# Attention and two feed-forward layers on one core: probabilities transposed in two halves of 64 queries

## The chip, the cores and the metric

The kernel runs on one core of one Trainium2 chip. The metric is the device time of one execution in microseconds (us); the kernel before takes 1026.38 us, the median of 3 runs (1026.12 to 1026.88).

## What is computed

Four batches of eight heads, 576 positions, head size 64. Attention keeps only the scores within `tau` of a row's largest, and its output feeds two feed-forward layers (512 to 2048 to 512) over the 2304 tokens; all of it in float32.

```python
scores = scale * (q @ k^T)
scores = where(scores >= max(scores) - tau, scores, -1e9)
attn   = softmax(scores) @ v              # x: 2304 tokens x 512
x = gelu_like(x @ w_in1) @ w_out1         # h / (1 + exp(-1.702 h))
x = mish(x @ w_in2) @ w_out2
```

## The kernel before, in words

**Attention.** A program of 72 groups. A "full" group is 128 queries of a pair of heads (two heads, 64 channels each, stacked on the 128 partitions); a "mix" group gathers the last 64 queries of the heads of two pairs. For a group TensorE computes the scores (line 628) into two two-bank PSUM tiles `sc`, one for each head, with 64 rows of the array for each head. VectorE scales them and takes the row's minimum (line 651, it also empties `sc`), GpSimd adds `tau` (line 655), ScalarE takes the exponential (line 658), and VectorE applies the mask and sums (line 661). The probabilities lie with queries on the partitions in `pair` (tiles `g0a` to `g3a` in the trace).

**Turning and the product.** The product with v contracts over keys, so the probabilities are transposed first. `turn` (from line 682) issues this for a group in three units: four transposes of 128 x 128 into bank `tb[0]`, four into `tb[1]` (both line 702), and one for the last keys of both heads into `tb[2]` (line 697). Each unit is followed by a ScalarE copy out of PSUM (line 717): 128x512, 128x512, 128x128, into `pm` (tiles `wout1a`, `wout2a`) and `pmt` (`g0a`, `g1a`). `product` (line 740) runs once for two full groups: 20 matmuls of 256 columns into one half of `tb[3]`, in an array shape of 128 rows by 64 columns, and a ScalarE copy (line 749). `product_mix` (line 765) does the same for a mix group with 64 columns, and its result is copied out by line 772.

**Three array shapes.** Scores use 64 rows x 128 columns of the array for each matmul (64x64 in mix groups), transposes 128x128, products 128x64. Every change between them is a change of the array's shape.

**The feed-forward layers.** 48 steps (24 a layer); a step has seven products of line 867 into `h` and 48 matmuls of lines 942 and 945 (layer 1) or 987 (layer 2). `h` lies in the banks of `sc` and can be opened only when the last scores are read. The weights arrive as 64-bit words and are converted on ScalarE, VectorE and GpSimd (lines 414 to 428), then split in two float32r parts (lines 481, 482, 486, 503, 504); the activations are split in the same way (lines 531, 556, 557, 561). The conversion of layer 1 is done once, in its first eight steps and ahead of them.

**What sets the order.** `Order` is a list scheduler written by hand. Every operation is added with an engine, a planned duration, the keys that it reads and writes, and a rank; the scheduler runs a small event model and issues each engine's instructions in the order that the model gives. `NUDGE` shifts the ranks of single operations by their number. `KEEP` and `TURN` are the model's preference for staying in an array shape (`mode`) and its charge for a change. Softmax work has the rank of its group; the conversion of weights and the loading of the first activations have late ranks, so on VectorE they fill what the softmax leaves open. Keys are per bank: an operation that writes `("tb", 0)` is put behind the copy that reads it.

```python
add("PE", n * 0.109, lambda bank=bank, cs=cs: tr(bank, cs),
    ps, [("tb", bank)], rank, steps=max(n, 2))
add("ACT", t_act(cols), lambda src=src, dst=dst: nc.scalar.copy(dst, src),
    [("tb", bank)], [kpn + (half,)], rank)
```

## Time and profile before

| what | value |
|---|---|
| median of 3 runs | 1026.38 us (1026.12 to 1026.88) |
| the profiled execution | 1026.8 us |
| its span in the trace | 1025.0 us |
| TensorE busy (PE) | 1018.3 us, 99% |
| VectorE busy (DVE) | 831.7 us, 81% |
| ScalarE busy (ACT) | 660.0 us, 64% |
| GpSimd busy (POOL) | 170.2 us, 17% |
| granted TensorE clock | 0.999 of full speed |

PE is matmuls and PEld the loads of their stationary operand, which overlap them. A matmul's recorded duration holds its way through the array, so several overlap and a busy PE row is no proof of an engine at its limit; the distance from one start to the next tells the pace. In the timeline of an engine, `x8` means eight instructions merged in one row, with the time from the first start to the last end. Attention fills the first 260 us or so, the feed-forward layers the rest.

### The profile page before, as it was taken

What the parts mean: (1) busy time and instruction counts of PE and PEld (TensorE: products, weight loads), DVE (VectorE), ACT (ScalarE), POOL (GpSimd) and SP (SyncE); (2) the same over time, 40 slices, a digit from 0 to 9 for tenths busy, and PEclk for the clock granted to TensorE, in tenths of its full rate; (3) what the DMA queues carried; (4) which work ended last, traced back from release to release, by engine and by line L of the source; (5) the groups of instructions that cost most, each with busy time, mean ns of one, the idle gap of its engine ahead of it and who ended that gap; (6) DMA issues with size and microseconds to landing.
All of it is one profiled execution on the core that took longest, in us unless ns stands there. A gap on an engine that the chain in (4) does not pass through costs nothing.

```text
span 1025.0 us, 17308 instructions
## 1 busy us (share of the span) xinstructions
PE 1018.3 (99%) x6362; PEld 866.5 (85%) x6362; DVE 831.7 (81%) x1642; ACT 660.0 (64%) x1262; POOL 170.2 (17%) x182
## 2 busy tenths in 40 slices
PE   9999999999999999999999999999999999999998
PEld 6666666666899999999999999989988998989897
DVE  6999999999889999888887788866597665985643
ACT  5888788888966778666777567644364444544430
POOL 2344444333221211112221012000000000000000
PEclk9999999999999999999999999999999999999999
DMA  5442437532246637755375543611135122131101
GB/s 198 135 137 76 142 117 244 175 96 76 87 154 200 205 122 262 245 209 197 110 273 192 206 171 101 220 64 62 63 104 164 62 73 72 62 124 62 42 1 62
DMA packets 55366, 137.52 MB, mean 134 GB/s; under 512 B 8433, under 2 KB 18673, under 8 KB 55281
## 3 DMA queue, kind: packets, MB, share of 16 engines
q1 hardware_dynamic: 55280, 136.41, 39.7%
q8 instruction: 50, 0.82, 0.3%
q14 instruction: 36, 0.29, 0.1%
HBM read 105.38 MB, written 31.01 MB: 133 GB/s over the span
## 4 chain that ended last, share of the span: by engine, by line
PE 97%; DVE 1%; ACT 1%; issue 0%; POOL 0%; POOLq 0%; DVEq 0%; ACTq 0%
PE h L867 34%; PE tb L987 13%; PE tb L942 13%; PE sc L628 8%; PE tb L740 7%; PE h L945 7%; PE h L987 6%; PE tb L702 6%; PE tb L697 1%; PE tb L765 1%; PE tb L579 1%; DVE win2a L651 0%; ACT wout1a L717 0%; ACT g2a L658 0%; DVE g0a L661 0%
## 5 line engine op out<-in xcount | busy, mean ns | idle before, releaser
L881 DVE TENSOR_TENSOR hs<-h,u 128x384 f32<-128x384 f32 x144 | 79.8, 554 | 88.9 <-PE h L867 55.6
L867 PE MATMUL h<-xq,win 128*128 128x384 f32 x672 | 131.9, 335 | 0.0
L867 PE MATMUL h<-xq,win2b 128*128 128x384 f32 x672 | 131.7, 335 | 0.0
L867 PE MATMUL h<-xq,win1b 128*128 128x384 f32 x672 | 131.1, 335 | 0.0
L867 PEld LDWEIGHTS h<-xq,win1b 128*128 128x128 f32 x672 | 116.2, 188 | 5.5 <-ACT u L889 0.3
L867 PEld LDWEIGHTS h<-xq,win2b 128*128 128x128 f32 x672 | 116.2, 188 | 5.4
L867 PEld LDWEIGHTS h<-xq,win 128*128 128x128 f32 x672 | 115.7, 188 | 5.0 <-ACT u L889 0.5
L651 DVE TENSOR_SCALAR_CACHE_REDUCE win2a<-sc,nqsc 128x576 f32<-128x576 f32 x144 | 112.0, 812 | 5.5 <-PE sc L628 5.1
L889 ACT COPY u<-h 128x384 f32<-128x384 f32 x144 | 68.7, 477 | 72.7 <-PE h L867 71.6
L884 ACT ACTIVATE hs<-hs 128x384 f32<-128x384 f32 x144 | 75.7, 526 | 60.3 <-DVE hs L881 58.9
L655 POOL TENSOR_SCALAR nm<-nm,tau_p 128x1 f32<-128x1 f32 x144 | 84.2, 586 | 159.8 <-DVE win2a L651 156.5
L628 PE MATMUL sc<-win1a 64*128 64x288 f32 (+3 forms) x672 | 90.3, 415 | 0.5 <-DVE win2a L651 0.5
L486 DVE TENSOR_TENSOR sv<-sv 128x256 f32<-128x256 f32 x192 | 80.3, 419 | 1.3
L426 POOL TENSOR_TENSOR sg<-sg,sr 128x1024 uint32<-128x1024 uint32 x16 | 42.5, 2655 | 215.0 <-DVE sg L423 125.1
L628 PEld LDWEIGHTS sc<-win1a 64*128 64x128 f32 (+1 forms) x672 | 50.9, 174 | 28.6 <-issue 10.0
L481 ACT CAST win1b<-sv 128x256 fp32r<-128x256 f32 (+1 forms) x96 | 42.0, 442 | 44.0 <-DVE sv L486 26.2
L481 ACT CAST win<-sv 128x256 fp32r<-128x256 f32 (+1 forms) x96 | 42.3, 443 | 38.4 <-DVE sv L486 26.8
L481 ACT CAST win2b<-sv 128x256 fp32r<-128x256 f32 (+1 forms) x96 | 42.2, 445 | 29.6 <-DVE sv L486 19.7
L482 DVE TENSOR_TENSOR win<-sv,win 128x256 fp32r<-128x256 f32 (+1 forms) x96 | 50.6, 532 | 10.4 <-ACT win L481 10.4
L426 POOL TENSOR_TENSOR sv<-sv,sr 128x1024 uint32<-128x1024 uint32 x16 | 43.0, 2685 | 79.0 <-DVE sv L423 44.7
L482 DVE TENSOR_TENSOR win1b<-sv,win1b 128x256 fp32r<-128x256 f32 (+1 forms) x96 | 48.2, 506 | 7.5 <-ACT win1b L481 7.3
L482 DVE TENSOR_TENSOR win2b<-sv,win2b 128x256 fp32r<-128x256 f32 (+1 forms) x96 | 46.3, 483 | 9.8 <-ACT win2b L481 9.5
(244 smaller groups left out, 2285.9 us busy)
## 6 DMA issues: line engine op xcount, KB each, us to landing
sv<-w_d SPq DMA_DIRECT2D x80, 512.0 KB
sr<-in_w_in SPq DMA_DIRECT2D x16, 1024.0 KB
sr<-in_w_out SPq DMA_DIRECT2D x32, 512.0 KB
win1a<-in_kq SPq DMA_DIRECT2D x16, 576.0 KB
xr<-x_d SPq DMA_DIRECT2D x24, 384.0 KB
w_d<-sv SPq DMA_DIRECT2D x16, 512.0 KB
w_d<-sg SPq DMA_DIRECT2D x16, 512.0 KB
x_d<-xo SPq DMA_DIRECT2D x16, 288.0 KB
```

Source lines behind the costliest of these rows:

```text
L426: lambda: nc.gpsimd.tensor_tensor(bits, bits, word(0), ALU.add), keys, [kval], rank, port=True)
L481: add("ACT", t_act(256 * m, psum=False), lambda: nc.scalar.copy(at(0), src), [ku] + pre_in, keys, rank)
L482: add("DVE", t_dve(256 * m), lambda: nc.vector.tensor_tensor(at(1), src, at(0), ALU.subtract), [ku], keys, rank, port=True)
L486: add("DVE", t_dve(256), lambda: nc.vector.tensor_tensor(out, x, y, op), [], [ku], rank, port=True)
L628: nc.tensor.matmul(sc[i][at:at + m, g, c0:c0 + n], kq2[rows, q0:q0 + m], kq2[rows, k0:k0 + n], start=True, stop=True)
L651: lambda: nc.vector.tensor_scalar(n3, s3, nqsc, None, ALU.mult, ALU.min, accum_out=nm[:, 0:1]),
L655: lambda: nc.gpsimd.tensor_scalar(nm[:, 1:2], nm[:, 0:1], tau_p, 0.0, ALU.add, ALU.add),
L867: nc.tensor.matmul(dst(), w[:, h, c], xq[p][:, x, cs], start=(start and i == 0), stop=(p in (5, 6) and i == 5), skip_group_check=True)
L881: add("DVE", t_dve(HALF), lambda: nc.vector.tensor_tensor(ht[:, cs], x(), y, ALU.add), [kx, ky], [kh + (j,)], rank - 4.0)
L884: lambda: nc.scalar.activation(ht[:, cs], x() if y is None else ht[:, cs], fn),
L942: nc.tensor.matmul(acc2[e](), w[:, x], g(y)[:, 0:512], start=first, stop=last, skip_group_check=True)
L987: nc.tensor.matmul(acc2[t](), g(x)[:, t * 128:(t + 1) * 128], w[:, y], start=(k == i == j == 0), stop=(k == KP - 1 and i == 1 and j == 2), ...
```

## The change

The nine transposes of a group become eighteen, each of 64 queries: half `r` reads 64 partitions of `pair` and multiplies by a 64 x 64 corner of the identity, so it uses the array in the shape of the scores (64 rows x 128 columns). The sixteen main ones are one unit, with the two halves in turn; half 0 goes to bank `tb[0]`, half 1 to `tb[1]`. The tail is a second unit, with its halves in `tb[2]` and `tb[3]`. The copies are two of 128x512 (in blocks of 64 queries) and two of 128x64. The results of the product go alternately to `tb[2]` and `tb[3]`, beside the tails; `pm` becomes two buffers of 2048 columns in place of four of 1024. The transposes get the scores' `mode` in the scheduler, and `NUDGE` is another table.

```diff
--- before.py
+++ after.py
@@ -44,36 +44,43 @@
 NUDGE = {
-    14: 7, 26: -2, 43: 53, 54: -34, 59: -17, 67: -3, 70: -1, 80: -3, 86: -5, 87: -32, 116: 49, 121:
...
+    10: 37, 16: 8, 37: -5, 46: -1, 53: -1, 55: -29, 62: 8, 66: -38, 73: 4, 83: 14, 85: 30, 93: -48,
...
 }
@@ -588,7 +595,7 @@
     nms = Ring(mpool, "nm", 8, [128, 2], F32)
     sms = Ring(mpool, "sm", 4, [128, 32], F32)
     rts = Ring(mpool, "rt", 2, [128, 32], F32)
-    pms = Ring(cut("wout", 1, 2, 1024) + cut("wout", 2, 2, 1024), "pm", 4)
+    pms = Ring([early["wout", 1], early["wout", 2]], "pm", 2)
     pmt = Ring([early["g", i][:, 1168:1424] for i in range(2)], "pmt", 2)
     xos = Ring(mpool, "xo", 3, [128, S], F32)
     xo = {}
@@ -688,34 +695,40 @@
             xo[b, hp] = xos.next()
         half = t % 2 if full else 0
         if not full or t % 2 == 0:
-            turned[b, hp] = [pms.next(), pms.next(), pmt.next()]
-        plan = [(0, (0, 1)), (1, (2, 3)), (2, (4,))]
-
-        def tr(bank, cs):
-            for n, c in enumerate(cs):
-                if c == 4:
-                    nc.tensor.transpose(tb[bank][:, 0:128], pair[:, 516:644], ident)
+            turned[b, hp] = [pms.next(), pmt.next()]
+        (pm, kpm), (rest, krest) = turned[b, hp]
+
+        def tr(out, at, r):
+            rows = slice(64 * r, 64 * r + 64)
+            nc.tensor.transpose(out, pair[rows, at:at + 128], ident[rows, rows])
+
+        def block(k, r):
+            tr(tb[r][:, 64 * k:64 * k + 64], (P1 + 64 if k % 2 else 4) + k // 2 * 128, r)
+
+        def main():
+            for k in range(8):
+                for r in range(2):
+                    block(k, r)
                     yield
-                    continue
-                for i in range(len(ps)):
-                    a, c0 = (P1 + 64 if i else 4) + c * 128, (n * len(ps) + i) * 128
-                    nc.tensor.transpose(tb[bank][:, c0:c0 + 128], pair[:, a:a + 128], ident)
-                    yield
-
-        for (bank, cs), (pn, kpn) in zip(plan, turned[b, hp]):
-            n = 1 if 4 in cs else len(ps) * len(cs)
-            cols = 128 * n
-            n = add("PE", n * 0.109, lambda bank=bank, cs=cs: tr(bank, cs),
-                ps, [("tb", bank)], rank, steps=max(n, 2))
-            if sch.fill is None and WARM:
-                sch.fill = ("PE", n, 0.107, keep_warm)
-            src = tb[bank][:, 0:cols]
-            dst = pn[:, 0:cols]
-            if full:
-                dst = pn.rearrange("p (g q) -> p g q", q=256)[:, :, half * 128:half * 128 + 128]
-                src = src.rearrange("p (g q) -> p g q", q=128)
-            add("ACT", t_act(cols), lambda src=src, dst=dst: nc.scalar.copy(dst, src),
-                [("tb", bank)], [kpn + (half,)], rank)
+
+        def tail():
+            for r in range(2):
+                tr(tb[2 + r][:, 0:64], 516, r)
+                yield
+
+        n = add("PE", 8 * 0.109, main, ps, [("tb", 0), ("tb", 1)], rank, steps=16, mode=1)
+        add("PE", 0.109, tail, ps, [("tb", 2), ("tb", 3)], rank, steps=2, mode=1)
+        if sch.fill is None and WARM:
+            sch.fill = ("PE", n, 0.107, keep_warm)
+        for r in range(2):
+            dst = pm.rearrange("p (g q) -> p g q", q=256)[:, :, half * 128 + 64 * r:half * 128 + 64 * r + 64]
+            src = tb[r].rearrange("p (g q) -> p g q", q=64)
+            add("ACT", t_act(512), lambda src=src, dst=dst: nc.scalar.copy(dst, src),
+                [("tb", r)], [kpm + (2 * half + r,)], rank)
+        for r in range(2):
+            at = half * 128 + 64 * r
+            add("ACT", t_act(64), lambda r=r, at=at: nc.scalar.copy(rest[:, at:at + 64], tb[2 + r][:, 0:64]),
+                [("tb", 2 + r)], [krest + (2 * half + r,)], rank)
         if not full:
             for i in range(2):
                 product_mix(b, hp - 1 + i, i, turned[b, hp], rank)
@@ -727,23 +740,24 @@
         _, b, hp, t = tl
         _, vr, _, kvr = head[b, hp]
         at = t // 2 * 256
-        pn = [p for p, _ in turned[b, hp]]
+        (pm, kpm), (rest, krest) = turned[b, hp]
         i = avn[0] % 2
         avn[0] += 1
-        av, kav = tb[3][:, i * 256:i * 256 + 256], ("tb", 3)
+        av, kav = tb[2 + i][:, 64:320], ("tb", 2 + i)
 
         def mm(cs):
             for c in cs:
                 for i in range(2):
-                    p, a = (pn[c // 2], (c % 2 * 2 + i) * 256) if c < 4 else (pn[2], 0)
+                    p, a = (pm, (c * 2 + i) * 256) if c < 4 else (rest, 0)
                     vc = c * 128 + 64 * i
                     nc.tensor.matmul(
                         av[64 * i:64 * i + 64], vr[:, vc:vc + 64], p[:, a:a + 256],
                         start=(c == 0), stop=(c == 4))
                     yield
 
-        for cs, (_, kp) in zip(((0, 1), (2, 3), (4,)), turned[b, hp]):
-            add("PE", len(cs) * 0.43, lambda cs=cs: mm(cs), [kp + (0,), kp + (1,), kvr], [kav, "product"],
+        for cs, kp in (((0, 1), [kpm + (i,) for i in range(4)]), ((2, 3), [kpm + (i,) for i in range(4)]),
+                       ((4,), [krest + (i,) for i in range(4)])):
+            add("PE", len(cs) * 0.43, lambda cs=cs: mm(cs), kp + [kvr], [kav, "product"],
                 rank + VR, steps=2 * len(cs), mode=2)
         x, kx = xo[b, hp]
         add("ACT", t_act(256), lambda: nc.scalar.copy(x[:, at:at + 256], av), [kav],
@@ -752,22 +766,23 @@
     def product_mix(b, hp, i, pn, rank):
 
         _, vr, _, kvr = head[b, hp]
-        av, kav = tb[2][:, 256 + 64 * i:320 + 64 * i], ("tb", 2)
+        (pm, kpm), (rest, krest) = pn
+        av, kav = tb[2][:, 320 + 64 * i:384 + 64 * i], ("tb", 2)
 
         def mm():
             for c in range(5):
                 for j in range(2):
                     q = 64 * (j ^ i)
                     if c < 4:
-                        p, a, vc = pn[c // 2][0], (c % 2 * 2 + i) * 128 + q, c * 128 + 64 * j
+                        p, a, vc = pm, (c * 2 + i) * 256 + q, c * 128 + 64 * j
                     else:
-                        p, a, vc = pn[2][0], q, 512 + 64 * (i if i == j else 2 + i)
+                        p, a, vc = rest, q, 512 + 64 * (i if i == j else 2 + i)
                     nc.tensor.matmul(
                         av[64 * j:64 * j + 64], vr[:, vc:vc + 64], p[:, a:a + 64],
                         start=(c == 0), stop=(c == 4))
                 yield
 
-        add("PE", 0.575, mm, [k + (0,) for _, k in pn] + [kvr], [kav], rank + VR, steps=5, mode=2)
+        add("PE", 0.575, mm, [kpm + (0,), kpm + (1,), krest + (0,), krest + (1,), kvr], [kav], rank + VR, steps=5, mode=2)
         x, kx = xo[b, hp]
         add("ACT", t_act(64), lambda: nc.scalar.copy(x[:, 512:S], av), [kav], [kx + (4,)], rank + VR)
         finish(b, hp, rank + VR)
@@ -829,7 +844,7 @@
     reopen("win", 1, [("kq", i) for i in range(3)])
     reopen("win", 2, [("ss", i) for i in range(NSS)])
     for i in range(2):
-        reopen("wout", 1 + i, [("pm", 2 * i), ("pm", 2 * i + 1)])
+        reopen("wout", 1 + i, [("pm", i)])
     for i in range(4):
         reopen("g", i, [("p", i)] + ([("pmt", i)] if i < 2 else []))
     for i in range(3):
```

## Rows read from the trace of the kernel before

**Rows 1.** The page: span, busy time by engine, and shares of the chain.

```profile
span 1025.0 us, 17308 instructions
PE 1018.3 (99%) x6362; PEld 866.5 (85%) x6362; DVE 831.7 (81%) x1642; ACT 660.0 (64%) x1262; POOL 170.2 (17%) x182
...
PE 97%; DVE 1%; ACT 1%; issue 0%; POOL 0%; POOLq 0%; DVEq 0%; ACTq 0%
```

**Rows 2.** Busy time by stretch: length, PE, PEld, DVE, ACT, POOL, clock, DMA share, GB/s.

```profile
20.00:40.00 20.00, 19.02 (x152) 11.98 (x151) 19.73 (x50) 17.68 (x32) 7.24 (x12) 1.00 0.17 59
40.00:240.00 200.00, 200.00 (x1753) 131.57 (x1752) 197.60 (x509) 167.35 (x337) 81.31 (x116) 1.00 0.43 141
240.00:280.00 40.00, 40.00 (x364) 29.95 (x363) 37.14 (x88) 36.40 (x75) 11.23 (x15) 1.00 0.31 90
280.00:400.00 120.00, 120.00 (x694) 112.45 (x693) 111.04 (x166) 85.96 (x150) 23.35 (x9) 1.00 0.55 180
400.00:480.00 80.00, 80.00 (x462) 74.72 (x461) 67.84 (x113) 57.07 (x107) 15.69 (x6) 1.00 0.64 217
```

**Rows 3.** Groups of VectorE instructions from 0 to 250 us.

```profile
L651 DVE TENSOR_SCALAR_CACHE_REDUCE win2a<-sc,nqsc 128x576 f32<-128x576 f32 x136 | 105.8, 812 | 5.5 <-PE sc L628 5.1
...
L428 DVE SCALAR_TENSOR_TENSOR sv<-sr,sv 128x1024 uint32<-128x1024 uint32 x6 | 7.3, 1214 | 0.0
L557 DVE TENSOR_TENSOR xq<-xr,xq 128x768 fp32r<-128x768 f32 x5 | 4.8, 952 | 0.0
```

**Rows 4.** TensorE timeline, 12 to 263 us: start, time, engine, line, operation.

```profile
12.05 1.24 PE L628 MATMUL sc<-win1a 64*128 64x288 f32 x8
13.22 1.09 PE L702 MATMUL tb<-ident,g0a 128*128 128x128 f32 x8
...
256.37 1.24 PE L628 MATMUL sc<-win1a 64*128 64x288 f32 x8
257.54 0.33 PE L697 MATMUL tb<-ident,g0a 128*128 128x128 f32 x1
257.70 1.04 PE L702 MATMUL tb<-ident,g0a 128*128 128x128 f32 x8
258.58 0.27 PE L697 MATMUL tb<-ident,g1a 128*128 128x128 f32 x1
258.78 1.08 PE L740 MATMUL tb<-wout1a,x22a 128*64 128x256 f32 x8
```

**Rows 5.** TensorE timeline, 262 to 270 us: products, transposes, feed-forward matmuls.

```profile
262.39 1.95 PE L740 MATMUL tb<-wout2a,x20a 128*64 128x256 f32 x16
264.17 0.60 PE L740 MATMUL tb<-g1a,x20a 128*64 128x256 f32 x4
264.70 0.33 PE L697 MATMUL tb<-ident,g2a 128*128 128x128 f32 x1
...
265.66 1.29 PE L867 MATMUL h<-xq,win 128*128 128x384 f32 x6
266.79 0.60 PE L702 MATMUL tb<-ident,g3a 128*128 128x128 f32 x4
267.22 0.27 PE L697 MATMUL tb<-ident,g3a 128*128 128x128 f32 x1
```

**Rows 6.** TensorE timeline, 272 to 274 us: a mix product, 64 columns a matmul.

```profile
272.43 0.69 PE L765 MATMUL tb<-wout2a,x22a 128*64 128x64 f32 x16
272.95 0.29 PE L765 MATMUL tb<-g1a,x22a 128*64 128x64 f32 x4
```

**Rows 7.** Loads of the stationary operand, from 120.82 us: the scores' first four.

```profile
120.82 0.30 PEld L628 LDWEIGHTS sc<-win1a 64*128 64x128 f32 x4 [0.39 <-DVE sv L420]
```

**Rows 8.** Groups of ScalarE instructions from 0 to 250 us.

```profile
L717 ACT COPY wout2a<-tb 128x512 f32<-128x512 f32 x66 | 37.1, 595 | 10.0 <-PE tb L702 9.7 <-ACT wout2a L717 0.2
...
L717 ACT COPY g0a<-tb 128x128 f32<-128x128 f32 x32 | 8.9, 278 | 2.7 <-PE tb L697 2.7
...
L772 ACT COPY xo<-tb 128x64 f32<-128x64 f32 x14 | 2.9, 210 | 1.5 <-PE tb L765 1.4
```

**Rows 9.** ScalarE timeline, 126 to 130 us: two copies, then two exponentials.

```profile
126.81 1.07 ACT L717 COPY wout2a<-tb 128x512 f32<-128x512 f32 x2
...
127.91 1.48 ACT L658 ACTIVATE g1a<-win2a,nm 128x576 f32<-128x576 f32 x2
```

**Rows 10.** The waits from 0 to 250 us: who, on whom, total us, times, longest.

```profile
PEld tb L702 <- ACT wout1a L717: 2.8, 7, 0.6
```

65 rows, old and new, of the table NUDGE are left out of this document.

## The prediction

> **What bounds the kernel now.** I read the page first. TensorE is busy for 99% of the span and holds 97% of the chain that ended last [rows 1]. That alone proves little, since recorded matmuls overlap, so I looked at starts in TensorE's timeline. Where a run of one kind ends, the next begins at once, and the same distance recurs [rows 4, 5]; the largest wait of a transpose on a copy sums to 2.8 us in the first 250 us [rows 10]. TensorE really has no holes there.
>
> The table by stretch shows a second full engine. From 40 to 240 us VectorE is busy for 197.60 of 200 us (98.8%) while the attention runs, and from 280 to 400 us, where the first eight feed-forward steps and the conversion of layer 1's weights lie, for 111.04 of 120 [rows 2]. The reader is to see that both engines are packed until about 400 us, and that only behind it (67.84 of 80 from 400 to 480) VectorE has room. Part of what VectorE does in the attention is filler: weight conversion and the first activations [rows 3], which are needed for the feed-forward steps and have been pulled forward. So time that TensorE gives back shows in the end only as far as VectorE can follow: its mandatory softmax must move closer together, and the filler must be done later.
>
> **The change part by part, TensorE.** A run of ten transposes starts at 257.54 and is followed by a product at 258.78: 1.24 us. Its middle eight take 0.88 from first start to the next kind's start, 0.110 each, so ten would be 1.10; the other 0.14 lie at the two ends, 0.07 an end [rows 4]. Where transposes follow feed-forward matmuls of the same 128x128 shape, four of them take 0.43, 0.108 each, and the first costs nothing extra [rows 5]. So what the ends cost is the change of shape. A change ends one run and begins another, two ends, 0.14 us, if the scores' ends cost what the transposes' do. I counted 65 changes between the scores' 64x128 and the transposes' 128x128 (24 of them from transposes back to scores), from the one ahead of 13.22 to the one ahead of 257.54 [rows 4]. With the new shape these go: 65 x 0.14 = 9.1 us. The others (transposes or products on one side, products or mix scores on the other) stay in this order; another order may have fewer, which I don't count.
>
> The transposes themselves: nine at 0.110 = 0.99 us a group become nine pairs. What a pair costs no row shows. It streams 64 columns in each half; in a mix product two 64-column matmuls side by side take 0.065 (eight pairs from 272.43 to 272.95) [rows 6]. That is the low end, 0.59 us a group, a gain of 0.40 or 29 us over 72 groups. The high end is that the two halves don't overlap and each keeps a transpose's pace, 0.22 a pair, a loss of 0.99 a group or 71 us. For overlap speak the scores, in the very shape that is used: their first four loads of a 64x128 operand take 0.30 us from first start to last end [rows 7], less than three transposes take, and eight matmuls of 288 columns take 1.17 [rows 4], 0.146 each against 0.110 for 128 columns in a transpose. I take 0.110 a pair, no gain and no loss, which is also what the scheduler charges, and between the ends it is close to the low one; the gain that may lie below it is one that VectorE would not let through (below).
>
> A rule speaks against this change. The Trainium skill, "TensorE: Matmul & The Clock Gate", section "LDWEIGHTS (loading the stationary operand)", says that a load costs its columns at 1.2 GHz whatever the number of rows, so a half-height load costs as much as a full one, 107 ns. Eighteen loads one behind the other would be 1.92 us a group by it, an estimate, and the sum would come out some 60 us slower; with the two row halves loaded side by side it would be 0.96, about what there is now. The overlap in [rows 7] speaks for the second.
>
> **ScalarE.** The two 512-column copies stay at 0.595 each; one of 128 columns (0.278) becomes two of 64 (0.210 by the copy of a mix result, the nearest row), 0.142 more a group, 10.2 us in all [rows 8]. ScalarE is busy for 167.35 of 200 us [rows 2], so 72 groups' addition fits, and I cost it at nothing; the cover is its 33 us of idle time there. Blocks of 64 queries in place of 128 may slow the copies; the bound is nothing to a tenth of two copies, 0.12 us a group, also inside the cover.
>
> **Order and buffers.** Before, the first copy ran while the second bank was filled. Now both banks fill together, so both copies begin at the end of the run, and the next run waits for both. Behind it on TensorE would stand scores, and behind these VectorE's first softmax step. Between two runs TensorE has a group's scores (1.17 us [rows 4]) and half of a product (20 matmuls from 262.39 to 264.70, so 1.16 [rows 5]), 2.33 together; two copies take 1.07 [rows 9]. That hides it, with 1.26 us to spare, and costs nothing in the forecast. The product's first quarter now needs all four copies of two groups rather than two; it is issued a group and a half later, so nothing waits. The tails and the results of products share `tb[2]` and `tb[3]`, but products have two banks in place of one; I set it at nothing. `pm` keeps its size. No DMA is added or moved by hand; VectorE's and GpSimd's instructions are the same in number and size.
>
> **VectorE's limit, and the sum.** VectorE idles 2.67 us from 20 to 240, 2.86 from 240 to 280 and 8.96 from 280 to 400 [rows 2]: 14.5 us is all that could go before its deadline work ends, the upper bound. At the density that it holds now (98.8%), the 365.5 us of work from 20 to 400 need 370.0, a gain of 10.0. But part of its idle time behind 280 is waiting for `h` in the feed-forward chain; if half of that stays, the gain is 2.4 (20 to 280 at that density) + 4.5 = 6.9. I take the middle, 8.5, just under the 9.1 that TensorE gives. The profiled execution took 1026.8 us, 1.8 around its span and 0.4 over the median: 1026.8 - 8.5 = 1018.3, which is 1017.9 against the median.
>
> **Rivals.**
> 1. *More comes through* (0.13). Pairs run at 0.065 and another order drops more changes, so TensorE has up to 38 us to give, and VectorE's filler moves behind 400 us. Then the bound is its idle time up to 480: 14.5 + 12.2 = 26.6 us [rows 2], so 1000 to 1012. For it: the mix product's pace. Against: weight conversions have their deadlines in those first steps.
> 2. *The gain is lost on the way* (0.12). TensorE finishes the attention earlier and then stands in the first feed-forward steps, because the filler that VectorE skipped is late for the weights of steps 1 to 7; or 64-query copies lengthen ScalarE's queue. The time is then 1022 to 1028. For it: VectorE's 92.5% from 280 to 400. Mostly within 0.2%.
> 3. *Both banks at once make TensorE wait* (0.10, slower). If ScalarE has two exponentials ahead of the two copies (1.48 us [rows 9]), bank and copies take 2.55, 0.22 over what TensorE has in between; 72 times is 16 us, less 9.1 is 7 slower: 1033. It decides as soon as the wait is over 9.1 / 72 = 0.13 us a group. Against: TensorE hardly waits for copies now [rows 10], and the scheduler sees this dependence.
> 4. *The halves don't overlap* (0.05, slower). 71 - 9 = 62 us slower, 1088; the change then doesn't do what its shape promises. The Trainium skill's rule on loads, above, is this case when the loads come one behind the other. Against it: [rows 7].
>
> **How the numbers follow.** The forecast has 0.60, with 1012 to 1022 for itself (all of VectorE's idle time down to a third of it). The range leaves out rivals 3 and 4 (0.15) and the far part of rival 1: 1006 to 1027. A measurement of this kernel tells about 0.2%, 2 us, from no change. Faster by more: the forecast, rival 1 and a part of rival 2, 0.78; within: the rest of rival 2, 0.07, and a sliver of rival 3, 0.08; slower: the others, 0.14.
>
> **What would show it.** Right: 18 transposes a group of 64x128 at 0.11 a pair or less, no extra 0.07 between scores and transposes, the first feed-forward matmul (265.66 now [rows 5]) some 6 to 10 us earlier, VectorE at 98 to 99% until about 390. If VectorE instead shows idle time in the attention with transposes as releaser, or transposes waiting for copies, rival 3 holds; if pairs start 0.22 apart, rival 4; if TensorE shows holes from 260 to 400, rival 2. My prediction is wrong if VectorE is no limit, that is, if the gain goes past 15 us, or if the attention gets no shorter although the shape changes are gone.

## The result, and the profile after

The changed kernel takes 1034.21 us (1033.06 to 1039.16 over 3 runs), 1.0086 times the kernel before, interval 1.0073 to 1.01. The forecast was 1017.9 us and faster; it is 8 us slower and lies outside the range. Line numbers have moved: scores 628 to 635, first softmax step 651 to 658, exponential 658 to 665, second step 661 to 668, transposes to 703, their copies to 726 (512 columns) and 730 (64), product 740 to 753 and its copy 749 to 763, mix product 765 to 780, feed-forward products 867 to 882 and 942 to 957.

The page after, against [rows 1]: span, busy time, chain, and the scores' group (busy, mean ns, then idle time before it and what ended it).

```profile
span 1032.4 us, 18739 instructions
PE 1003.7 (97%) x7010; PEld 859.3 (83%) x7010; DVE 829.5 (80%) x1642; ACT 662.9 (64%) x1334; POOL 168.0 (16%) x182
...
PE 82%; DVE 7%; ACT 6%; issue 3%; DMA 2%; DVEq 0%; POOL 0%; SPq 0%; ACTq 0%; POOLq 0%
...
L635 PE MATMUL sc<-win1a 64*128 64x288 f32 (+3 forms) x672 | 107.4, 415 | 14.8 <-DVE win2a L658 14.2
```

TensorE's share of the chain fell from 97% to 82%, and VectorE and ScalarE have come in. The same stretches as in [rows 2]:

```profile
20.00:40.00 20.00, 17.23 (x190) 10.54 (x188) 17.69 (x48) 18.42 (x37) 7.84 (x13) 1.00 0.18 61
40.00:240.00 200.00, 182.96 (x2199) 123.35 (x2198) 195.90 (x499) 165.16 (x379) 77.74 (x115) 1.00 0.45 145
240.00:280.00 40.00, 37.09 (x432) 26.29 (x428) 37.19 (x96) 34.61 (x87) 9.29 (x14) 1.00 0.25 76
280.00:400.00 120.00, 120.00 (x724) 111.34 (x721) 101.29 (x156) 88.03 (x153) 26.74 (x10) 1.00 0.48 160
400.00:480.00 80.00, 80.00 (x463) 74.88 (x462) 69.66 (x110) 56.48 (x106) 15.34 (x6) 1.00 0.62 216
```

The second column is TensorE, the fourth VectorE. From 40 to 240 us TensorE now has 17.0 us of idle time and had none; VectorE has 4.1 us where it had 2.4. Over 20 to 280 us VectorE's idle time grew from 5.5 to 9.2 us. TensorE was relieved and the attention got no shorter. The waits from 0 to 290 us say where TensorE's new idle time lies (the forms of [rows 10]):

```profile
PEld sc L635 <- DVE win2a L658: 29.9, 56, 2.5
...
PE sc L635 <- DVE win2a L658: 14.2, 20, 2.4
...
PEld tb L703 <- ACT wout1a L726: 3.0, 7, 1.3
...
PE tb L753 <- ACT g1a L730: 2.3, 2, 1.2
...
PE tb L703 <- ACT xo L763: 2.2, 4, 0.8
```

Before, from 0 to 250 us, the first of these was

```profile
PEld sc L628 <- DVE win2a L651: 6.7, 20, 0.8
```

Scores wait for VectorE to empty the bank, 29.9 us at the loads and 14.2 at the matmuls. Transposes waiting for the copies of the probabilities stay as small as they were (3.0 us here, 2.8 before, in the largest row of each). Two waits are new and smaller: products for the copies of the tails (line 730, 2.3 us), and transposes for the copies of products (line 763, 2.2 us), with which they now share banks. TensorE's timeline after, near the end of the attention:

```profile
254.89 0.67 PE L703 MATMUL tb<-ident,g1a 64*128 64x64 f32 x16
255.39 0.37 PE L703 MATMUL tb<-ident,g0a 64*128 64x64 f32 x2
256.79 1.97 PE L635 MATMUL sc<-win1a 64*128 64x288 f32 x8 [1.02 <-DVE win2a L658]
...
267.43 2.36 PE L882 MATMUL h<-xq,win 128*128 128x384 f32 x12
...
277.94 0.66 PE L703 MATMUL tb<-ident,g3a 64*128 64x64 f32 x16
278.69 1.95 PE L753 MATMUL tb<-wout1a,x20a 128*64 128x256 f32 x16
280.47 0.60 PE L753 MATMUL tb<-g0a,x20a 128*64 128x256 f32 x4
...
285.70 0.69 PE L780 MATMUL tb<-wout2a,x20a 128*64 128x64 f32 x16
286.22 0.29 PE L780 MATMUL tb<-g1a,x20a 128*64 128x64 f32 x4
286.44 0.50 PE L957 MATMUL tb<-g0b,wout 128*128 128x512 f32 x1
```

And before, the same places:

```profile
269.20 0.60 PE L740 MATMUL tb<-g0a,x20a 128*64 128x256 f32 x4
...
275.45 0.69 PE L765 MATMUL tb<-wout2a,x20a 128*64 128x64 f32 x16
...
280.50 0.39 PE L942 MATMUL tb<-g0b,wout 128*128 128x512 f32 x1
```

Sixteen half transposes from 254.89 are followed by the next kind at 255.39: 0.50 us, eight pairs at 0.062. The first feed-forward product starts at 267.43 (265.66 in [rows 5]), 1.8 later. But the last product of full groups reaches its last four matmuls at 280.47 where it reached them at 269.20, 11.3 later, and the last mix product starts at 285.70 instead of 275.45, 10.3 later. The first output matmul (line 957, 942 before) needs the hidden products of its step, which TensorE does between these remains of the attention; it starts at 286.44 instead of 280.50, 5.9 later.

To say where time goes I read the same events from each kernel's timelines (us): the start of the last first softmax step (A, line 651 or 658), the last second step (B), the first feed-forward product (H), the first output matmul (O), the first output matmul of the ninth step, behind layer 1's conversion (O9), and the last output matmul of all (E).

| kernel | A | B | H | O | O to O9 | O9 to E |
|---|---|---|---|---|---|---|
| before | 262.8 | 265.2 | 265.7 | 280.5 | 127.1 | 613.4 |
| after | 263.7 | 270.8 | 267.4 | 286.4 | 127.2 | 614.7 |
| b_plain | 265.8 | 268.3 | 268.8 | 285.3 | 130.1 | 615.1 |
| b_merge_plain | 269.0 | 275.0 | 271.1 | 291.3 | 127.7 | 615.6 |
| b_sf4_plain | 266.4 | 268.9 | 269.4 | 285.9 | 129.8 | 614.8 |
| a_plain | 268.5 | 277.8 | 269.3 | 293.7 | 123.9 | 617.0 |
| a_cost_plain | 258.7 | 265.9 | 261.3 | 280.5 | 132.8 | 616.9 |
| a_sf4_plain | 260.1 | 263.4 | 261.0 | 278.6 | 133.3 | 617.5 |
| a_half_plain | 257.5 | 266.4 | 259.9 | 279.7 | 135.1 | 616.9 |
| a_cost_ranked | 258.0 | 263.4 | 258.8 | 277.0 | 126.7 | 616.8 |
| a_sf4_ranked | 260.4 | 265.1 | 261.3 | 280.1 | 126.1 | 614.7 |

Of the 7.3 us by which E comes later after the change, 5.9 lie ahead of O, 0.1 between O and O9, and 1.3 behind. Ahead of O the first softmax steps end almost when they did (0.9 later); the rest is a longer tail behind them. The mean distance from a group's first to its second softmax step (each time the later of its two) grew from 3.7 to 7.3 us, and from there to the product (from the second of its two full groups) from 6.9 to 10.4. So the attention is a pipeline of almost the same pace that has become 7.1 us deeper, and a deeper pipeline takes longer to run empty: behind A there are 74 half transposes (four groups) and 60 product matmuls of full groups left, before it was 18 transposes (two groups) and 36. From A to O, before and after:

```profile
262.84:280.50 17.66, 17.66 (x151) 14.98 (x147) 14.98 (x35) 17.01 (x36) 3.86 (x3) 1.00 0.29 93
263.73:286.44 22.71, 21.78 (x229) 16.37 (x223) 19.18 (x46) 22.51 (x55) 1.92 (x3) 1.00 0.11 36
```

TensorE is all but full there, and ScalarE, with the copies and exponentials of those groups, is busy for 22.51 of 22.71 us; so what is left of the attention holds up the feed-forward steps. H, O and O9 say when one kind of work first starts, and the order decides what is done around them; only A and E tell how far the whole has come.

### The profile page after: what moved, and what is told of

It is laid out like the page before. It is cut to its first block, busy times and chain, and to the rows that moved or that the text cites. A ratio compares the mean times of both kernels' runs of the same rounds, so it can differ in the third digit from the quotient of the medians.

```text
span 1032.4 us, 18739 instructions
## 1 busy us (share of the span) xinstructions
PE 1003.7 (97%) x7010; PEld 859.3 (83%) x7010; DVE 829.5 (80%) x1642; ACT 662.9 (64%) x1334; POOL 168.0 (16%) x182
## 4 chain that ended last, share of the span: by engine, by line
PE 82%; DVE 7%; ACT 6%; issue 3%; DMA 2%; DVEq 0%; POOL 0%; SPq 0%; ACTq 0%; POOLq 0%
PE h L882 33%; PE tb L1002 13%; PE tb L957 12%; PE h L1002 6%; PE h L960 6%; PE sc L635 5%; PE tb L753 4%; DVE win2a L658 3%; PE tb L703 2%; DMA sr<-in_w_in 1%; ACT g2a L665 1%; ACT wout1a L726 1%; ACT g1a L665 1%; DVE g3a L668 1%; ACT wout2a L726 1%
## 5 line engine op out<-in xcount | busy, mean ns | idle before, releaser
L635 PE MATMUL sc<-win1a 64*128 64x288 f32 (+3 forms) x672 | 107.4, 415 | 14.8 <-DVE win2a L658 14.2
L635 PEld LDWEIGHTS sc<-win1a 64*128 64x128 f32 (+1 forms) x672 | 60.1, 174 | 41.6 <-DVE win2a L658 29.9
L493 DVE TENSOR_TENSOR sv<-sv 128x256 f32<-128x256 f32 x192 | 84.1, 439 | 1.4
L488 ACT CAST win<-sv 128x256 fp32r<-128x256 f32 (+1 forms) x96 | 42.3, 444 | 44.8 <-DVE sv L493 29.9
L489 DVE TENSOR_TENSOR win2b<-sv,win2b 128x256 fp32r<-128x256 f32 (+1 forms) x96 | 49.8, 522 | 9.9 <-ACT win2b L488 9.5
```

The lines of the kernel that those rows point to most:

```text
L488: add("ACT", t_act(256 * m, psum=False), lambda: nc.scalar.copy(at(0), src), [ku] + pre_in, keys, rank)
L489: add("DVE", t_dve(256 * m), lambda: nc.vector.tensor_tensor(at(1), src, at(0), ALU.subtract), [ku], keys, rank, port=True)
L493: add("DVE", t_dve(256), lambda: nc.vector.tensor_tensor(out, x, y, op), [], [ku], rank, port=True)
L635: nc.tensor.matmul(sc[i][at:at + m, g, c0:c0 + n], kq2[rows, q0:q0 + m], kq2[rows, k0:k0 + n], start=True, stop=True)
```

## The experiments

There were two questions: which engine carries the attention now, and what made the pipeline deeper. Each ratio is against the kernel before, run on the same chip (medians of 1026.4 to 1027.4 us).

### Which engine carries it

**pe_before** and **pe_after**: more tail transposes and nothing else, into the same columns. They are repeated work and change no value.

```diff
-                    nc.tensor.transpose(tb[bank][:, 0:128], pair[:, 516:644], ident)
+                    for _ in range(3):
+                        nc.tensor.transpose(tb[bank][:, 0:128], pair[:, 516:644], ident)
...
-            for r in range(2):
-                tr(tb[2 + r][:, 0:64], 516, r)
-                yield
+            for n in range(10):
+                tr(tb[2 + n % 2][:, 0:64], 516, n % 2)
+                if n > 7:
+                    yield
```

> The kernel before, same order, with the tail transpose of each group issued three times in place of once: 144 more transposes at 0.11 us, 15.8 us more for TensorE in the attention, and nothing else. If TensorE sets the pace of the attention before: 12 to 16 us slower. If VectorE does as well, so that both have to wait for neither: still close to that, as TensorE has no room. If TensorE has room: under 4 us.

> The changed kernel, same order, with the tail's pair of half transposes issued five times in place of once: 288 more pairs at 0.062 us, 17.9 us more for TensorE. If the change did free TensorE and something else now sets the pace: under 6 us slower than the changed kernel (under 1040). If TensorE still sets it: 14 to 18 us slower (1048 to 1052).

**dve_before** and **dve_after**: the first clamp of a weight's conversion is issued twice on VectorE.

```diff
-            lambda: nc.vector.tensor_scalar(val, val, cmin, cmax, ALU.max, ALU.min),
+            lambda: [nc.vector.tensor_scalar(val, val, cmin, cmax, ALU.max, ALU.min) for _ in range(2)],
```

> The kernel before, same order, with the first clamp of each converted weight block issued twice: 16 more VectorE instructions of 0.65 us before 400 us, 6 of them in the attention, 10.4 us in all; 16 more later, where VectorE has room. If VectorE's work up to 400 us bounds the kernel: 5 to 10 us slower. If TensorE alone does: under 3 us.

> The changed kernel with the same doubled clamp. If the attention has become VectorE's alone and what TensorE gave back is lost there: 5 to 10 us slower than the changed kernel (1039 to 1044). If the drain behind the last softmax step is what costs, VectorE's work counts less: 1 to 5 us (1035 to 1039).

Measured: pe_before 1040.64 us, ratio 1.0131 (1.0114 to 1.0148); pe_after 1035.51, 1.008 (1.0065 to 1.0095); dve_before 1044.71, 1.0172 (1.0151 to 1.0194); dve_after 1054.3, 1.0269 (1.0249 to 1.0289). First what was added. Timeline of pe_before:

```profile
100.40 0.55 PE L698 MATMUL tb<-ident,g3a 128*128 128x128 f32 x3
100.78 1.04 PE L703 MATMUL tb<-ident,g3a 128*128 128x128 f32 x8
```

Timeline of pe_after:

```profile
102.25 0.47 PE L703 MATMUL tb<-ident,g3a 64*128 64x64 f32 x10
102.55 0.67 PE L703 MATMUL tb<-ident,g0a 64*128 64x64 f32 x16
```

The longer tails take 0.38 us (three transposes) and 0.30 us (five pairs) up to the next start; at the 0.110 of [rows 4] two more transposes a group are 144 x 0.110 = 15.8 us, and at 0.062 four more pairs are 288 x 0.062 = 17.9. Before, 13.2 of the 15.8 came through (1040.64 against 1027.42). After, 17.9 us of TensorE work move the ratio from 1.0086 to 1.008: nothing. Both lie in the range expected for a TensorE that sets the pace before and is relieved after. The table by stretch of pe_after shows who took them in:

```profile
40.00:240.00 200.00, 189.89 (x2616) 135.01 (x2614) 195.34 (x498) 164.18 (x376) 77.53 (x114) 1.00 0.45 143
```

TensorE is busy 189.89 us instead of 182.96 and VectorE as before; the holes swallowed them. So TensorE is no limit in the changed attention. That VectorE is, the clamps show. The row of line 427 in dve_after (minimum, median and longest in ns, first and last start):

```profile
L427 DVE TENSOR_SCALAR sv<-sv x32: 679/693/2770, 25.3 to 380.2; 128x1024 f32<-128x1024 f32 x32
L427 DVE TENSOR_SCALAR sg<-sg x32: 677/694/1302, 417.4 to 661.1; 128x1024 f32<-128x1024 f32 x32
```

Half of these are added, 32 x 0.69 = 22.1 us on VectorE, the same in both kernels. The cost was 17.3 us before and, by the ratios, 18.8 after (1.0269 against 1.0086; the medians of two chips, 1054.3 and 1034.21, are 20.1 apart). Both are about twice the 5 to 10 us that were expected. Only six of the added clamps lie ahead of A, so the sum does not tell about the attention; the stages do. From 20 us to A, in the changed kernel and in dve_after:

```profile
20.00:263.73 243.73, 221.94 (x2656) 148.73 (x2652) 236.96 (x605) 202.12 (x460) 93.79 (x140) 1.00 0.42 133
20.00:270.54 250.54, 225.62 (x2663) 150.32 (x2662) 244.28 (x613) 202.90 (x461) 94.33 (x140) 0.99 0.40 129
```

VectorE is busy for 7.3 us longer and A comes 6.8 later; between dve_before and the kernel before it is 3.7 and 3.2. In pe_before A comes 12.6 us later, in pe_after 1.7. So ahead of A both engines carry the time in the kernel before, and VectorE does after the change. The rest of what the clamps cost (in the profiled executions 15.9 us before, 11.8 after) comes behind A. In dve_before TensorE has 5.8 us of holes between O and O9, where it had none, though VectorE idles for 11.7 of those 138.9 us: a busy share does not tell what a wait there costs.

### What made it slower

The two kernels differ in their rank tables too, so the parts are compared with an empty table first, before and after alike.

**b_plain**, **a_plain**: the kernels as they are, `NUDGE = {}`.

> The kernel before with an empty table of rank shifts, so that the list scheduler's bare order runs; the base for the next three. Banks theory (the change is slow because one run of transposes fills both banks and the next run must wait for two copies): some 1030 to 1038, as the shifts of before are worth a few us. Ranks theory (the new table is simply a worse one, the structure is sound): the same here, and the changed kernel with an empty table comes out equal or faster than this one.

> The changed kernel with an empty table. Banks theory: 5 to 9 us slower than the kernel before with an empty table, about the 7.8 that separate the two with their tables. Ranks theory: equal to it or faster, down to 8 us faster.

**b_merge_plain**: b_plain with one part of the change alone. The old 128x128 transposes fill both banks as one unit, then both copies follow.

```diff
-        plan = [(0, (0, 1)), (1, (2, 3)), (2, (4,))]
+        plan = [((0, 1), (0, 1, 2, 3)), ((2,), (4,))]
...
-            n = add("PE", n * 0.109, lambda bank=bank, cs=cs: tr(bank, cs),
-                ps, [("tb", bank)], rank, steps=max(n, 2))
+            n = add("PE", n * 0.109, lambda banks=banks, cs=cs: tr(banks, cs),
+                ps, [("tb", x) for x in banks], rank, steps=max(n, 2))
```

> The kernel before with an empty table, and with its two units of four transposes made one unit of eight that fills both banks, then both copies; array shape, transposes and product as before. Banks theory: 5 to 8 us slower than the kernel before with an empty table, the distance from a group's first softmax step to its second grows from under 4 us to 6 or more, and the last product ends later by more than the last softmax step does. Ranks theory: within 2 us of it, since nothing of the shape or of the ranks differs.

**a_cost_plain**: a_plain with the scheduler's charge for a pair at what the trace shows.

```diff
-        n = add("PE", 8 * 0.109, main, ps, [("tb", 0), ("tb", 1)], rank, steps=16, mode=1)
-        add("PE", 0.109, tail, ps, [("tb", 2), ("tb", 3)], rank, steps=2, mode=1)
+        n = add("PE", 8 * 0.062, main, ps, [("tb", 0), ("tb", 1)], rank, steps=16, mode=1)
+        add("PE", 0.062, tail, ps, [("tb", 2), ("tb", 3)], rank, steps=2, mode=1)
```

> The changed kernel with an empty table, and with the scheduler's charge for a pair of half transposes at 0.062 us, the pace that the trace shows, in place of 0.109. The instructions are the same, only their order can differ. Charge theory (the order is planned for transposes that take almost twice what they do): 4 to 7 us faster than the changed kernel with an empty table. Banks theory alone: within 3 us of it, since the wait is for copies and not for TensorE.

Measured: b_plain 1035.6 us, ratio 1.0084 (1.0069 to 1.0099); a_plain 1040.3, 1.0133 (1.0116 to 1.015); b_merge_plain 1038.77, 1.0117 (1.0102 to 1.0132); a_cost_plain 1036.53, 1.0104 (1.0083 to 1.0126). Three things follow, each a little short of what its theory gave.

The tables aren't the whole reason: without them the change still costs 4.7 us (1040.3 against 1035.6; the banks theory had 5 to 9) of the 7.8. Each kernel's table is worth 6 to 9 us, the one of before the more.

One unit for both banks costs 3.2 us by itself (5 to 8 were expected), in the old array shape, where TensorE gains nothing. Its distances are those of the changed kernel: first to second softmax step 6.3 us on the mean (b_plain 3.6), second step to product 10.5 (5.9), and H to O is 20.2 us instead of 16.5. That is not a longer end alone: A comes 3.2 later as well, and 2.4 us come back between O and O9. From 20 to 262 us VectorE waits for scores, which the waits of b_plain do not show at all:

```profile
DVE win2a L620 <- PE sc L597: 3.0, 6, 1.2
```

With the right charge the kernel is 3.8 us faster than a_plain (4 to 7 were expected, and the intervals of the two ratios overlap), and the order uses more of what TensorE gives: A comes at 258.7, 7.1 us ahead of b_plain's 265.8, as the forecast wanted. For that, VectorE does less filler in the attention: its work other than the two softmax steps, added up over all instructions ahead of A, is 41.0 us and in b_plain 45.8 (42.6 in the kernel before, 44.7 in the changed one). Yet the whole is no faster than b_plain. More of the attention is left behind A: 74 half transposes and 56 product matmuls of full groups, as many groups as in the changed kernel; in b_plain 23 transposes, two and a half groups, and 36. Of 7.5 us at H, 2.7 go between H and O (19.2 against 16.5), 2.7 between O and O9, and 1.8 behind. Between H and O VectorE does what was put off, it is busy for 18.1 of 19.1 us (13.0 of 16.6 in b_plain). The stretch from 280 to 400 us shows the part behind O. b_plain:

```profile
40.00:240.00 200.00, 198.18 (x1721) 132.10 (x1722) 197.20 (x506) 165.08 (x330) 72.14 (x115) 1.00 0.45 144
...
280.00:400.00 120.00, 118.16 (x676) 110.03 (x676) 104.36 (x156) 85.57 (x148) 25.67 (x10) 1.00 0.47 156
```

a_cost_plain:

```profile
40.00:240.00 200.00, 183.86 (x2234) 125.15 (x2233) 198.13 (x512) 167.67 (x383) 73.87 (x117) 1.00 0.42 132
...
280.00:400.00 120.00, 115.14 (x682) 106.10 (x678) 104.71 (x154) 82.73 (x142) 29.14 (x10) 0.99 0.51 172
...
395.00:400.00 5.00, 3.14 (x13) 2.99 (x13) 5.00 (x9) 2.68 (x6) 0.00 (x0) 0.81 1.03 397
```

TensorE has 4.9 us of holes there (1.8 in b_plain); from 395 to 400 us VectorE is full (5.00 of 5) and TensorE has 3.14. Its hole there, 1.86 us, ends with VectorE's addition for `hs`, which stood behind 1.8 us of splitting the next activations. So VectorE is late at this place. That it is so because of the filler that was put off isn't shown: over the whole stretch it is as busy as in b_plain (104.71 and 104.36 us). The granted clock fell besides, to 0.81 here and 0.84 in the next 5 us; by these shares that is 1.7 us, an estimate.

**a_sf4_plain**, **b_sf4_plain**: scores are ranked 4 groups ahead of their transposes rather than 8, in a_cost_plain and in b_plain.

```diff
-SF = 8
+SF = 4
```

> The changed kernel with an empty rank table and the charge of 0.062 us a pair (1036.5 us), and one constant changed: scores are ranked 4 groups ahead of their transposes and products, no longer 8. Theory, drain: the changed kernel is slow because scores and first softmax steps run further ahead of second steps and products, so that more is left to do behind the last first step. Ranked closer, the mean distance from first to second softmax step falls from 5.5 towards 4 us, the time between the first feed-forward product and the first output product from 19.1 to 16 to 17.5 us, and the time to 1032 to 1035. Rival, bank unit: the distance is set by the unit that fills two banks before either is copied, whatever the rank; distance, stretch and time stay, 1035 to 1038. Rival, starvation: VectorE lacks scores in the attention, its busy share from 40 to 240 us falls under 97%, and the time goes over 1039.

> The kernel before with an empty rank table (1035.6 us) and the same constant, 4 groups in place of 8. Theory, drain: its distance from first to second softmax step is already 3.6 us, so there is little to shorten: 1034 to 1037, and the stretch between the first feed-forward product and the first output product stays at 16 to 17 us. Rival, bank unit: the same here. Rival, starvation: over 1039, and less VectorE in the attention.

Measured: a_sf4_plain 1035.03 us (1033.01 to 1035.12), ratio 1.0074 (1.006 to 1.0088); b_sf4_plain 1036.58, 1.0097 (1.0083 to 1.0111). The stages came as the drain theory wanted: first to second softmax step 5.5 to 4.0 us, H to O 19.2 to 17.6, and nothing changes in b_sf4_plain (3.6 us and 16.5). The time is at the edge of what it gave and 1.5 us below a_cost_plain, whose interval it touches. The other half of the depth does not depend on the rank: from second step to product it is 8.7 and 8.2 us, against 5.9 in b_plain, so the rival holds for that part. b_sf4_plain came as both theories had it. And of the 1.9 us won ahead of O, 1.1 are spent again behind it. Stretches of a_sf4_plain:

```profile
364.00:368.00 4.00, 3.47 (x21) 2.87 (x19) 3.97 (x5) 1.23 (x3) 2.49 (x1) 1.00 0.00 0
368.00:372.00 4.00, 2.70 (x10) 2.06 (x11) 4.00 (x8) 3.01 (x6) 0.00 (x0) 0.89 0.43 173
372.00:376.00 4.00, 3.43 (x12) 2.92 (x11) 3.11 (x5) 0.60 (x2) 0.00 (x0) 0.50 0.98 231
```

VectorE is full, TensorE waits, and then its granted clock (the seventh number) is at half. It is the pattern of a_cost_plain, in other steps.

### Looking for a version that keeps the gain

**a_half_plain**: a_cost_plain with the sixteen transposes in two units, each into one half of both banks, and four copies of 256 columns, so that copies can start earlier; a product's quarters wait for the half that they read.

```diff
-        n = add("PE", 8 * 0.062, main, ps, [("tb", 0), ("tb", 1)], rank, steps=16, mode=1)
+        for u in range(2):
+            n = add("PE", 4 * 0.062, lambda u=u: main(u), ps, [("tb", r, "ab"[u]) for r in range(2)], rank,
+                    steps=8, mode=1)
```

> The changed kernel with an empty table, the pair's charge at 0.062, and the run of sixteen half transposes split in two units of eight, each into one half (256 columns) of both banks, with four copies of 128x256 in place of two of 128x512; so a later unit waits only for the copies of its own half. Banks theory: 4 to 8 us faster than the same without the split (1036.5), and products start sooner after a group's last softmax step (8.7 us there). Charge theory alone: within 2 us of it, or slower by the extra fixed cost of the copies.

**a_cost_ranked**, **a_half_ranked**, **a_sf4_ranked**: a_cost_plain, a_half_plain and a_sf4_plain with a rank table searched for each.

> The changed kernel with the pair's charge at 0.062 and a new table of rank shifts, searched for that charge in the scheduler's own model. If the loss lies in the order alone (charge and ranks): 1022 to 1029, that is equal to the kernel before or a little faster. If the structure (both banks at once) costs whatever the order: 1031 or more.

> The version with half-bank units, the charge of 0.062 and a table searched for it in the same way and for as long. Banks theory: faster than the one without half-bank units by 3 to 6 us, and faster than the kernel before, 1018 to 1024. Ranks theory alone: equal to the one without them.

> The changed kernel with the charge of 0.062, scores ranked 4 ahead and a rank table searched for just this (152 entries). Theory, drain: ranks were worth 9 us to the same kernel with 8, so from 1032 to 1035 about 1023 to 1027, level with the kernel before or up to 3 us faster. Rival, bank unit: the ranks had found their way round the distance already, 1026 to 1029 as with 8. Rival, starvation: over 1030.

Measured: a_half_plain 1040.97 us, ratio 1.0137 (1.012 to 1.0153); a_half_ranked 1046.32, 1.0184 (1.017 to 1.0197); a_cost_ranked 1027.37, 1.0011 (1.0003 to 1.002); a_sf4_ranked 1026.8, 1.0005 (0.9996 to 1.0014).

The half banks failed: 4.4 us slower than a_cost_plain where 4 to 8 faster was expected, and over 20 above the range with a table. TensorE's timeline of a_half_ranked:

```profile
47.65 0.48 PE L688 MATMUL tb<-ident,g1a 64*128 64x64 f32 x2 [0.26 <-ACT wout1a L714]
48.36 0.40 PE L688 MATMUL tb<-ident,g1a 64*128 64x64 f32 x6 [0.23 <-ACT wout1a L714]
49.27 0.46 PE L688 MATMUL tb<-ident,g1a 64*128 64x64 f32 x7 [0.51 <-ACT wout2a L714]
50.20 0.36 PE L688 MATMUL tb<-ident,g1a 64*128 64x64 f32 x1 [0.46 <-ACT wout2a L714]
...
51.75 2.16 PE L620 MATMUL sc<-win1a 64*128 64x288 f32 x8
```

The sixteen transposes, one run elsewhere, are torn into pieces that wait for ScalarE's copies, 1.46 us in all. I had planned the halves of a bank as if they were free of each other. The copies say that the waits go by the whole bank:

```profile
48.85 0.37 ACT L714 COPY wout2a<-tb 128x256 f32<-128x256 f32 x1 [0.54 <-PE tb L688]
49.77 0.37 ACT L714 COPY wout2a<-tb 128x256 f32<-128x256 f32 x1 [0.55 <-PE tb L688]
```

The last two pieces (seven and one) are the second unit of their group, and each starts 0.05 us after one of these copies ends. The copies bring that same group's first unit into its buffer `wout2a`, out of the other half of the banks, and by the plan the second unit needs none of them. Whether the program or the chip sets these waits was not tried. Behind it the clock falls, and eight scores take 2.16 us (1.24 in [rows 4]). The two stretches:

```profile
50.00:52.00 2.00, 1.80 (x23) 1.57 (x25) 1.10 (x3) 1.49 (x6) 0.08 (x1) 0.56 0.00 0
52.00:54.00 2.00, 2.00 (x12) 1.10 (x14) 0.53 (x3) 0.75 (x2) 0.00 (x0) 0.59 0.57 106
```

With a bank as the unit, the right charge and a table for it, the changed kernel comes level with the kernel before and no further. a_cost_ranked lies in the range given for a loss in the order alone, and under the 1031 of a structure that costs whatever the order; a_sf4_ranked lies where the drain theory (1023 to 1027) and its rival (1026 to 1029) overlap and decides nothing. The new tables are of another kind, 152 shifts of 168 (a_cost_ranked) and 146 (a_sf4_ranked) on the mean against 360 of 18 in the changed kernel, and no run has such a table with the charge of 0.109: how much came of the charge and how much of the table is not told apart. a_sf4_ranked, as in [rows 2]:

```profile
40.00:240.00 200.00, 184.33 (x2262) 126.63 (x2260) 198.56 (x509) 172.00 (x393) 73.91 (x117) 1.00 0.42 135
...
280.00:400.00 120.00, 120.00 (x694) 112.10 (x692) 110.64 (x161) 88.02 (x151) 29.25 (x11) 1.00 0.57 189
```

VectorE is at 99.3% in the attention, TensorE has 15.7 us to spare there, and O (280.1), O to O9 (126.1) and O9 to E (614.7) are the kernel before's within 1.3 us. No version here beats it.

## Why the prediction was wrong

**What bounds the kernel** was right in its words: two packed engines, and a gain that shows only as far as VectorE follows. pe_before and dve_before confirm both for the attention.

**TensorE** was right in its direction and too low in size. The half transposes overlap: a pair takes 0.062 us, the low end (0.065 by the mix product), not the 0.110 that I took. The Trainium skill, "TensorE: Matmul & The Clock Gate", section "LDWEIGHTS (loading the stationary operand)", says otherwise: at 107 ns for 128 columns even halves loaded side by side would give 0.107 a pair, an estimate. The trace of the changed kernel has sixteen loads in 0.58 us, and the measurement decides:

```profile
254.84 0.58 PEld L703 LDWEIGHTS tb<-ident,g1a 64*128 64x128 f32 x16
```

TensorE got 17 us of air from 40 to 240 us alone. How much of it is the 9.1 us for shape changes no run separates (of the 65 that were counted 22, not 24, lead from transposes back to scores; the sum is the same).

**ScalarE** held: from 40 to 240 us it runs 379 instructions in place of 337, is busy for 165.16 of 200 us, and the added copies hide. The shared banks `tb[2]` and `tb[3]`, set at nothing, brought the two new waits above, 2.3 and 2.2 us; beside the 14.2 us in which scores wait for VectorE they decide nothing.

**"Hides it ... and costs nothing"**, on both banks being filled together, is the first step that failed. I looked for a wait of TensorE on the copies in every group, as rival 3 did, and there is none to speak of. I should have asked how long a group's probabilities lie between the second softmax step and the product. That distance is paid at the end, where four groups in place of two are still to be copied, turned and multiplied behind A, on a ScalarE and a TensorE that are full. b_merge_plain prices the unit at 3.2 us, and shows that it costs in the steady run too: A comes later, and VectorE waits 3.0 us for scores. H to O grew by 4.2 in the changed kernel (14.8 to 19.0). a_sf4_plain shows that the scores' running ahead is another part.

**"VectorE's limit, and the sum"** is the second, and the bigger one: 8.5 us were to come out of VectorE's idle time, and the kernel became 7.8 us slower. VectorE was at 98.8% already; of what it idled from 20 to 262 us, 1.2 us were waits for scores, and its idle time became more (5.5 to 9.2 us over 20 to 280). The forecast needed filler moved out of the attention and took for granted that it has room behind. Where an order did that (a_cost_plain, 7.1 us earlier at A) the gain was gone by the end: more attention was left behind A, VectorE was full from H to O, and 3 us more of holes and 1.7 us of lower clock came behind it. That is near rival 2, which had 0.12; that the conversion as such was late for the steps isn't shown. I had the row for it, VectorE at 92.5% from 280 to 400, and counted its 9 us as a gain without asking whether TensorE waits for that time at all: in the kernel before it has no hole there.

**The charge** is the third. The text says that 0.110 "is also what the scheduler charges" and stops there. An order planned with a charge of 0.109 for what takes 0.062 does not know of the difference. From a_plain to a_cost_plain it is 3.8 us, in intervals that overlap, and A moves by 9.8; with the right charge and a table for it (a_cost_ranked) all of the loss but 0.1% is gone.

The signs named for a wrong prediction ("the attention gets no shorter although the shape changes are gone") are what the trace shows. Slower stood at 0.14, most of it rival 3: the right part of the change, the wrong mechanism, and a price of 7 us that agrees by chance.

What is left open: how the 7.8 us divide between unit, charge and table, since each was tried without the others' best; why the searched tables leave the changed structure exactly level with the old one; and what a_half_ranked's 20 us are. The granted clock of its stretches gives 5.1 us of them, an estimate of the most that full speed would have saved; the torn runs were not tried alone.

## What to carry to other kernels

Where two engines are both packed, relieving one is worth nothing unless the other's work in that stretch gets less; add work to each in turn and see which one pays, before believing a busy share. Merging a producer's units can leave the wait that one looks for as small as it was and still cost time, in another engine's waits and at the end, so measure how long data lie between their maker and their user, and what the run-out holds up. When an operation gets faster under a scheduler with planned durations, its charge has to be changed with it.

## What the runs showed of the hardware that was not expected

Transposes of 64 rows in the two halves of the array run side by side in full: 0.062 us a pair of 64 queries, where one 128x128 transpose takes 0.110. By these paces the nine blocks of a group take 0.56 us in place of 0.99.

Four holes of 0.2 to 0.5 us within 3 us, each a wait for a copy, were followed by a granted clock of 0.56 and 0.59 in the next two stretches of 2 us (a mix of 1.2 and 2.4 GHz), in a_half_ranked's attention, which falls twice more (0.62 from 80 to 84 us, 0.63 from 136 to 140) and holds 0.95 or more in all other stretches of 4 us. The changed kernel's attention has holes as well, scores wait up to 2.4 us and from 196 to 200 us TensorE is busy for 2.01 of 4, and it holds 1.00 in every stretch of 4 us. In a_sf4_plain holes of 0.4 to 0.9 us around 368 to 373 us were followed by 0.50, the level of 1.2 GHz.
